# Attention and two mixtures on one core: K's two split parts on the two halves of one tile's partitions, Q doubled by DMA

## Chip, core and metric

The kernel runs on one core of a Trainium2 chip. The metric is the device time of one execution in microseconds. Before the change the median of 3 runs is 985.72 us (985.22 to 987.43).

## What is computed

Sliding-window attention with sinks (4 batches, 8 heads, 768 positions, 64 columns a head), then a layer of three competing products, then a routed mixture of eight experts:

```python
scores = q @ k.T / sqrt(64)                      # kept: first 4 positions, and the last 128 up to the own one
x = softmax(scores) @ v                          # 4 x 8 x 768 x 64, rearranged to 3072 x 512
x = max(x @ w1, x @ w2, x @ w3) @ w_out          # first mixture, 512 -> 768 -> 512
logits = x @ w_gate                              # 8 experts, room for 384 tokens each, greedy by logit
out[mask_e] = relu(x[mask_e] @ u1[e]) @ u2[e]    # second mixture, 512 -> 1024 -> 512
```

All inputs are float32.

## The kernel before

The attention is cut into 32 units: a batch, a half of its 768 positions, and a pair of heads (4 x 2 x 4). Four units make a group, one group of 384 tokens for the first mixture, eight groups in all. A unit goes through four functions: `load` (transfers of K, Q, V and the sinks, all issued on SP's queue), `prep` (lines 83 to 109), `score` (110 to 137) and `soft`, and `pv` (138 to 184). On the partitions lie the two heads of the pair, 64 rows each: head 0 on partitions 0 to 63, head 1 on 64 to 127. In the code `a` is a head's own half of the partitions, `o` the other half.

The first eight units are native: they use float32 matmuls as they are (L123) and nothing in `prep` but the sinks. The other 24 are split units. There each operand is cut into a rounded part (float32r) and a remainder, and a product is made as rounded times rounded, plus remainder times rounded, plus rounded times remainder. For the scores of a head before the change:

- `KH[h]` (tile kh) holds rounded K on both halves of the partitions: two copies on ACT (L94), from `u['kn']`.
- `KZ[h]` (tile kz, kz0b, kz1b) holds K's remainder on half `a`, zeros on half `o`: a subtract on DVE (L95). The zeros are written once, by POOL (L53).
- `QS[h]` (tile qs) holds rounded Q on half `a` (ACT, L96) and Q's remainder on half `o` (DVE, L97), from `u['qn']`.
- The scores (L126, L127) are two matmuls into one accumulator with the same stationary operand, a 128 x 128 slice of `QS[h]`: times `KH[h]`, then times `KZ[h]`. A unit has six such pairs (three query blocks, two heads), 24 units have 144 pairs. The moving operand has 260 columns, or 132 in a first block.

After that the scores go to the tile T by a copy on ACT (L134) and a masked copy on DVE (L130, L135); softmax follows on ACT, DVE and POOL; `pv` turns the probabilities on TensorE (L25), masks them on DVE (L163), splits them (L176 on ACT, L177 on POOL) and multiplies by V (L181, L182).

K tiles kh and kz have one buffer at first, and a second one after the sixth `o` step, when an extra pool becomes free (L659 to L662); qs has two throughout; kn and qn have one each, so the transfers for the next unit wait until `prep` has read them (L75 and L77 on SP's queue, then V and sinks, L79 and L81).

The first mixture: `group` (L280 on TensorE, L282, L283, L288, L289 on ACT and DVE) makes the hidden layer of a group, `x2` (L305) its output. The hidden layer of the first group is spilled to memory and read back by `reload` on SP's queue (L321), split again on ACT (L323) and DVE (L324), and multiplied in L305 between groups 1 and 2.

What sets the order: all of this stands in one block whose instructions a planner puts in order by a simulated timeline with estimated durations. The code gives it a sequence of steps (`order`, `order1`, `spread`) and higher priority to the units of the next group and to evacuations. Each engine and each queue then runs its own list strictly in that order. The second mixture (from 601 us) stands outside of this block.

## Time and profile before

| | |
|---|---|
| median of 3 runs | 985.72 us (985.22 to 987.43) |
| profiled execution, its own time | 985.81 us |
| its span in the trace | 984.0 us |
| TensorE matmuls busy | 937.8 us (95%), 6552 instructions |
| VectorE (DVE) | 687.8 us (70%) |
| ScalarE (ACT) | 533.8 us (54%) |
| GpSimd (POOL) | 348.8 us (35%) |
| SP's hardware queue | 40560 packets, 71.57 MB |
| chain that ended last | TensorE 75%, DVE 8%, ACT 6%, issue 5%, DMA 4% |

Lines such as L126 are lines of the kernel before. In the profile PE is TensorE, PEld its weight loads, and a releaser (`<-`) is what ended an idle time. Matmuls are pipelined: their recorded durations overlap, so that the distance between two of them is shorter than one of them. A chain lists, in order of time, the pieces of work that the end hung on.

### The profile page before, as it was taken

The page shows a single profiled execution, that of the slowest core. Times are in us where ns is not written, and L with a number is a line of the kernel's source. Part 1 is how long each engine was busy: PE and PEld are TensorE (multiplying, and loading weights), DVE is VectorE, ACT ScalarE, POOL GpSimd, SP SyncE. Part 2 cuts the span into 40 slices and gives each one's busy share as a digit, 9 for nine tenths or more (in the row PEclk, how much of TensorE's full clock was granted, in tenths as well). Part 3 has the DMA queues.
Part 4 walks back from the last instruction along what each step waited for, and adds up shares of the span by engine and source line. Part 5 has one row for each costly group of instructions (what it writes and reads, how often), then busy time and mean ns, then how long its engine had stood idle before and what let it go on. Part 6 is the DMA issues. An engine that isn't in the chain of part 4 may idle for free.

```text
span 984.0 us, 18469 instructions
## 1 busy us (share of the span) xinstructions
PE 937.8 (95%) x6552; PEld 857.8 (87%) x6552; DVE 687.8 (70%) x1807; ACT 533.8 (54%) x1425; POOL 348.8 (35%) x317
## 2 busy tenths in 40 slices
PE   5889999969999999999999999999999999999996
PEld 4568989959999999999999998888888888888895
DVE  3897676687879976776764344879989889873320
ACT  4666664788789777677663211233433434344431
POOL 3578357145555535425434000011113032043331
PEclk8899999989999999999999999999999999999999
DMA  7455121222112112112110002544345352454420
GB/s 226 151 170 172 50 77 64 68 83 88 53 40 78 52 49 73 28 48 81 64 50 12 1 1 76 164 154 130 119 149 174 98 172 99 160 189 154 135 81 32
DMA packets 50541, 95.03 MB, mean 97 GB/s; under 512 B 6704, under 2 KB 20784, under 8 KB 50448
## 3 DMA queue, kind: packets, MB, share of 16 engines
q1 hardware_dynamic: 40560, 71.57, 23.4%
q0 software_dynamic: 3840, 12.45, 3.6%
q10 hardware_dynamic: 6048, 9.83, 2.7%
q8 instruction: 51, 0.84, 0.4%
q14 instruction: 42, 0.34, 0.1%
HBM read 77.84 MB, written 16.12 MB: 95 GB/s over the span
## 4 chain that ended last, share of the span: by engine, by line
PE 75%; DVE 8%; ACT 6%; issue 5%; DMA 4%; POOL 1%; SPq 1%; POOLq 0%; ACTq 0%; DVEq 0%
PE mm L280 28%; PE mm L608 11%; PE acc L601 11%; PE mm L305 7%; PE po L181 3%; PE rc L406 2%; PE pt L25 2%; PE pp L25 2%; PE po L172 2%; PE ps L126 1%; PE ps L127 1%; DMA sa<-in_u_dram 1%; PE ps L123 1%; DVE A_w L163 1%; DVE qs L97 1%
## 5 line engine op out<-in xcount | busy, mean ns | idle before, releaser
L601 PE MATMUL acc<-wbh,HL 128*128 128x512 f32 x384 | 131.1, 398 | 0.0
L177 POOL TENSOR_TENSOR L<-A_w,H 128x768 fp32r<-128x768 f32 x46 | 87.0, 1891 | 101.5 <-ACT H L176 91.1
L283 DVE TENSOR_TENSOR hm<-mm,hm 128x384 f32<-128x384 f32 x96 | 53.3, 555 | 68.6 <-PE mm L280 65.1
L620 POOL DMA_INDIRECT out_dram<-og,idx x24 | 32.2, 1340 | 180.6 <-ACT og L619 177.3
L305 PE MATMUL mm<-woh,HL 128*128 128x260 f32 (+1 forms) x432 | 89.5, 296 | 2.0 <-DVE HL L324 1.1
L552 ACT ACTIVATE wah<-sa 128x512 fp32r<-128x512 f32 x64 | 40.5, 632 | 89.6 <-PE mm L608 72.2
L601 PEld LDWEIGHTS acc<-wbh,HL 128*128 128x128 f32 x384 | 71.5, 188 | 12.8
L552 ACT ACTIVATE wbh<-sb 128x512 fp32r<-128x512 f32 x64 | 40.4, 631 | 74.9 <-PE acc L601 72.0
L601 PE MATMUL acc<-wbl,HL 128*128 128x512 f32 x192 | 76.9, 401 | 0.0
L305 PEld LDWEIGHTS mm<-woh,HL 128*128 128x128 f32 x432 | 72.3, 198 | 3.3 <-DVE HL L324 1.4
L608 PE MATMUL mm<-HL,wah 128*128 128x384 f32 x256 | 68.5, 343 | 0.0
L280 PE MATMUL mm<-xh,w0h 128*128 128x384 f32 x192 | 66.8, 348 | 1.2 <-ACT xh L267 0.6
L280 PE MATMUL mm<-xh,w1h 128*128 128x384 f32 x192 | 66.7, 347 | 0.8 <-ACT hm L282 0.5
L280 PE MATMUL mm<-xl,w0h 128*128 128x384 f32 x192 | 65.5, 341 | 1.9 <-DVE xl L268 1.9
L280 PE MATMUL mm<-xh,w2h 128*128 128x384 f32 x192 | 67.0, 349 | 0.0
L280 PE MATMUL mm<-xh,w1l 128*128 128x384 f32 x192 | 65.5, 341 | 0.0
L280 PE MATMUL mm<-xl,w2h 128*128 128x384 f32 x192 | 65.5, 341 | 0.0
L553 DVE TENSOR_TENSOR wbl<-sb,wbh 128x512 fp32r<-128x512 f32 x64 | 43.9, 688 | 30.7 <-ACT wbh L552 30.7
L280 PE MATMUL mm<-xl,w1h 128*128 128x384 f32 x192 | 65.1, 339 | 0.0
L280 PE MATMUL mm<-xh,w0l 128*128 128x384 f32 x192 | 65.1, 339 | 0.0
L280 PE MATMUL mm<-xh,w2l 128*128 128x384 f32 x192 | 65.1, 339 | 0.0
L612 DVE SCALAR_TENSOR_TENSOR HL<-mm,HL 128x384 fp32r<-128x384 f32 x64 | 35.5, 554 | 40.8 <-ACT HL L611 40.6
(320 smaller groups left out, 2888.3 us busy)
## 6 DMA issues: line engine op xcount, KB each, us to landing
sa<-in_u_dram SPq DMA_DIRECT2D x64, 256.0 KB
sb<-in_u_dram SPq DMA_DIRECT2D x64, 256.0 KB
HL<-in_words_dram SPq DMA_DIRECT2D x18, 512.0 KB
qn<-in_q_dram SPq DMA_DIRECT2D x24, 192.0 KB
x2d<-xo ACTq DMA_DIRECT2D x15, 256.0 KB
kn<-in_k_dram SPq DMA_DIRECT2D x12, 264.0 KB
st<-in_words_dram SPq DMA_DIRECT2D x6, 512.0 KB
vn<-in_v_dram SPq DMA_DIRECT2D x12, 256.0 KB
```

The source lines that it names most:

```text
L25: nc.tensor.transpose(out,x,f32(ident))
L177: nc.gpsimd.tensor_tensor(L,Af,f32(H),op=OP.subtract)
L181: nc.tensor.matmul(po[:,q:q+n],u['VS'][:,blk,128*h:128*h+128],part[:,c:c+n],start=(part is H and j==0),stop=False,skip_group_check=True)
L280: nc.tensor.matmul(ps[:,:384],s.W[i][a][:,p,f*128:(f+1)*128],X[p][b],start=(n==0),stop=(n==11)); n+=1
L283: else: nc.vector.tensor_tensor(m,ps[:,:384],m,op=OP.max)
L305: nc.tensor.matmul(ps[:,:n],H[f][a][:,t*128:(t+1)*128],s.WO[b][:,f,u,c],start=(k==0),stop=(k==17)); k+=1
L552: nc.scalar.activation(h,src,AF.Copy)
L553: (nc.gpsimd if s.n>=6 and nm=="wa" else nc.vector).tensor_tensor(l,src,f32(h),op=OP.subtract)
L601: s.mms.append(nc.tensor.matmul(acc[t],H[f][a][:,t*128:(t+1)*128],W[f][1][b],start=(f==0 and n==0),stop=(f==F-1 and n==2))); n+=1
L608: s.mms.append(nc.tensor.matmul(ps[:,:384],W[f][0][a][:,k,:],X[k][b],start=(n==0),stop=(n==11))); n+=1
L612: nc.vector.scalar_tensor_tensor(l,ps[:,:384],0.0,f32(h),op0=OP.max,op1=OP.subtract)
L620: st=nc.gpsimd.indirect_dma_start(out=s.out,out_offset=bass.IndirectOffsetOnAxis(ap=idx[:,t:t+1],axis=0),in_=o,in_offset=None)
```

## The change

Rounded K and its remainder now stand in one tile `KK[h]` (the tiles kh): rounded on half `a`, by one ACT copy, and the remainder on half `o`, by the DVE subtract, which now writes across the halves. Q of a head is loaded twice, to both halves, so that one unit has four transfers of 64 x 384 in place of one of 128 x 384; one ACT copy over all 128 partitions rounds it into `QS[h]`. A new tile `QL[h]` holds Q's remainder on half `a` beside zeros on half `o`; it has one buffer at first and a second one after the sixth `o` step, as KZ had. The two matmuls of a pair now have the same moving operand, `KK[h]`, and two stationary ones, `QS[h]` and `QL[h]`. The zeros that POOL writes are 64 x 384 in place of 64 x 528. For native units only a name changes.

```diff
--- before.py
+++ after.py
@@ -44,7 +44,7 @@
         for i in range(2):
             t=consts.tile([128,2,128],FR,name=f"vk{i}"); nc.vector.memset(f32(t),0.0); s.vk.append(t)
             t=consts.tile([128,384],FR,name=f"psb{i}"); nc.vector.memset(f32(t),0.0); s.pb.append(t)
-        s.kf=[]; s.kz=[s.zeros([consts.tile([128,4,132],FR,name=f"kz{h}") for h in range(2)])]
+        s.kf=[]; s.ql=[s.zeros([consts.tile([128,384],FR,name=f"ql{h}") for h in range(2)])]
         t=consts.tile([1,1],FT,name="one"); nc.vector.memset(t,0.0)
         nc.scalar.activation(t,t,AF.Exp)
         s.n=0; s.no=('kh0','kh1')
@@ -65,16 +65,17 @@
         half=[(slice(64*h,64*h+64),slice(64-64*h,128-64*h)) for h in range(2)]
 
         if native:
-            u['KZ']=s.kf[u['n']%len(s.kf)]
-            for h,(a,o) in enumerate(half): nc.sync.dma_start(u['KZ'][h][a,:nb],s.k[i,a,:nb*132].rearrange("d (c j) -> d c j",j=132))
+            u['KK']=s.kf[u['n']%len(s.kf)]
+            for h,(a,o) in enumerate(half): nc.sync.dma_start(u['KK'][h][a,:nb],s.k[i,a,:nb*132].rearrange("d (c j) -> d c j",j=132))
             u['QF']=w.tile([128,384],FT,name="qf",tag="qs0",bufs=2)
             nc.sync.dma_start(u['QF'],s.q[i])
             u['vn']=w.tile([128,4,2,64],FT,name="vnn",tag="vsp")
         else:
             u['kn']=w.tile([128,4,132],FT,name="kn",bufs=1)
             nc.sync.dma_start(u['kn'][:,:nb],s.k[i,:,:nb*132].rearrange("p (c j) -> p c j",j=132))
-            u['qn']=w.tile([128,384],FT,name="qn",bufs=1)
-            nc.sync.dma_start(u['qn'],s.q[i])
+            u['qn']=[w.tile([128,384],FT,name=f"qn{h}",bufs=1) for h in range(2)]
+            for h,(a,o) in enumerate(half):
+                for r in (a,o): nc.sync.dma_start(u['qn'][h][r],s.q[i,a])
             u['vn']=w.tile([128,4,2,64],FT,name="vn",bufs=1)
         nc.sync.dma_start(u['vn'][:,:nb],s.v[i].rearrange("t (c h d) -> t c h d",h=2,d=64)[:,:nb])
         u['sv']=w.tile([40,2,64],FT,name="vns",bufs=1)
@@ -84,18 +85,18 @@
         nc=s.nc; w=s.w; nb=u['nb']; nat=u['nat']
         half=[(slice(64*h,64*h+64),slice(64-64*h,128-64*h)) for h in range(2)]
         if not nat:
-            KZ=s.kz[u['n']%len(s.kz)]
-            KH=[s.two(u,[128,4,132],FR,f"kh{h}") for h in range(2)]
+            KK=[s.two(u,[128,4,132],FR,f"kh{h}") for h in range(2)]
             QS=[w.tile([128,384],FR,name=f"qs{h}",bufs=2) for h in range(2)]
+            QL=s.ql[u['n']%len(s.ql)]
             fl=nb*132
             flat=lambda t: t.rearrange("p c j -> p (c j)")[:,:fl]
             for h,(a,o) in enumerate(half):
                 k=flat(u['kn'])[a]
-                for r in (a,o): nc.scalar.activation(flat(KH[h])[r],k,AF.Copy)
-                nc.vector.tensor_tensor(flat(KZ[h])[a],k,f32(flat(KH[h])[a]),op=OP.subtract)
-                nc.scalar.activation(QS[h][a,:],u['qn'][a],AF.Copy)
-                nc.vector.tensor_tensor(QS[h][o,:],u['qn'][a],f32(QS[h][a,:]),op=OP.subtract)
-            u.update(KH=KH,KZ=KZ,QS=QS)
+                nc.scalar.activation(flat(KK[h])[a],k,AF.Copy)
+                nc.vector.tensor_tensor(flat(KK[h])[o],k,f32(flat(KK[h])[a]),op=OP.subtract)
+                nc.scalar.activation(QS[h],u['qn'][h],AF.Copy)
+                nc.vector.tensor_tensor(QL[h][a],u['qn'][h][a],f32(QS[h][a]),op=OP.subtract)
+            u.update(KK=KK,QS=QS,QL=QL)
         VK=u['VK']=s.vk[u['n']%2]
         hi,lo=(bass.AP(tensor=VK.tensor,offset=VK.offset+o,ap=[[VK.ap[0][0],40],[st,2],[1,64]]) for o,st in (((0,64),(128,64)) if nat else ((0,192),(64,64))))
         nc.gpsimd.tensor_copy(hi,u['sv'])
@@ -119,12 +120,11 @@
             t=T[:,2*i:2*i+2,:].rearrange("p u j -> p (u j)")
             for h in range(2):
                 ps=s.pss.tile([128,512],FT,name="ps")
-                iq=slice(i*128,(i+1)*128); kz=u['KZ'][h].rearrange("p c j -> p (c j)")[:,lo:lo+n]
+                iq=slice(i*128,(i+1)*128); kz=u['KK'][h].rearrange("p c j -> p (c j)")[:,lo:lo+n]
                 if u['nat']: nc.tensor.matmul(ps[:,:n],u['QF'][:,iq],kz,start=True,stop=True)
                 else:
-                    kh=u['KH'][h].rearrange("p c j -> p (c j)")[:,lo:lo+n]
-                    nc.tensor.matmul(ps[:,:n],u['QS'][h][:,iq],kh,start=True,stop=False)
-                    nc.tensor.matmul(ps[:,:n],u['QS'][h][:,iq],kz,start=False,stop=True)
+                    nc.tensor.matmul(ps[:,:n],u['QS'][h][:,iq],kz,start=True,stop=False)
+                    nc.tensor.matmul(ps[:,:n],u['QL'][h][:,iq],kz,start=False,stop=True)
                 block=t[:,136*h:136*h+128]; sink=t[:,128+4*h:132+4*h]
                 if first:
                     nc.vector.copy_predicated(block,s.ca[:,0,:],ps[:,0:128])
@@ -659,7 +659,7 @@
                     if n==5:
                         conv.release()
                         A.extra=A_("extra",1,side="right"); A.no=('A',)
-                        A.kz.append(A.zeros([A.extra.tile([128,4,132],FR,name=f'kz{h}b') for h in range(2)]))
+                        A.ql.append(A.zeros([A.extra.tile([128,384],FR,name=f'ql{h}b') for h in range(2)]))
             for o in order.split(): emit(o,False)
             rest=None
             for g in range(NG):
```

## Rows read from the trace of the kernel before

**Rows 1.** busy time by stage: start:end, length, busy us and instructions of each engine, TensorE's clock, DMA

```profile
0.00:50.00 50.00, 35.21 (x137) 23.95 (x137) 31.16 (x81) 29.60 (x105) 22.96 (x37) 0.83 0.62 187
196.00:225.00 29.00, 20.77 (x120) 18.37 (x119) 25.93 (x44) 25.73 (x82) 13.51 (x9) 0.77 0.34 101
225.00:540.00 315.00, 311.29 (x2111) 305.80 (x2110) 229.43 (x431) 231.55 (x671) 146.87 (x124) 1.00 0.17 54
```

**Rows 2.** TensorE's waits from 196 to 225 us: total, times, longest

```profile
PE ps L126 <- DVE T_w L135: 4.3, 3, 2.0
PE pp L25 <- DVE A_w L163: 1.2, 1, 1.2
PE mm L305 <- DVE HL L324: 1.1, 1, 1.1
```

**Rows 3.** timeline of ACT from 196 to 225 us: start, duration, instruction, idle before

```profile
200.94 1.31 ACT L94 ACTIVATE kh_w<-kn 64x528 fp32r<-64x528 f32 x2
202.28 0.28 ACT L134 ACTIVATE T_w<-ps 128x132 f32<-128x132 f32 x1
```

**Rows 4.** timeline of DVE in the same stretch

```profile
201.62 1.50 DVE L95 TENSOR_TENSOR kz<-kn,kh_w 64x528 fp32r<-64x528 f32 x1 [0.22 <-ACT kh_w L94]
203.04 0.28 DVE L135 COPY_PREDICATED T_w<-ca,ps 128x128 f32<-128x128 uint8 x1
...
204.21 0.55 DVE L97 TENSOR_TENSOR qs<-qn,qs 64x384 fp32r<-64x384 f32 x1
...
212.63 0.55 DVE L324 TENSOR_TENSOR HL<-hm,HL 128x384 fp32r<-128x384 f32 x1
...
215.66 1.91 DVE L95 TENSOR_TENSOR kz0b<-kn,kh_x 64x528 fp32r<-64x528 f32 x1 [0.36 <-ACT kh_x L94]
```

**Rows 5.** chain that ended last, three pieces after the stall, one at 302 us

```profile
212.71 0.12 PE ps L127
212.83 0.12 PE ps L126
...
222.47 4.97 PE mm L305 x30
...
302.28 4.31 PE mm L305 x36
```

**Rows 6.** instructions by line and shape: busy us, mean ns, idle before

```profile
L96 ACT ACTIVATE qs<-qn 64x384 fp32r<-64x384 f32 x48 | 24.8, 517 | 0.6
...
L267 ACT ACTIVATE xh<-x 128x384 fp32r<-128x384 f32 x32 | 15.6, 517 | 4.0 <-PE mm L280 3.4 <-DVE x L184 0.4
L94 ACT ACTIVATE kh_x<-kn 64x528 fp32r<-64x528 f32 x24 | 15.4, 642 | 2.8 <-PE ps L126 2.4
L94 ACT ACTIVATE kh_w<-kn 64x528 fp32r<-64x528 f32 x24 | 15.4, 642 | 0.8 <-PE ps L126 0.4
...
L127 PEld LDWEIGHTS ps<-kz,qs 128*128 128x128 f32 x78 | 14.9, 191 | 0.0
L94 ACT ACTIVATE kh_w<-kn 64x396 fp32r<-64x396 f32 x28 | 14.9, 531 | 3.8 <-PE ps L126 3.4
...
L94 ACT ACTIVATE kh_x<-kn 64x396 fp32r<-64x396 f32 x20 | 10.7, 533 | 3.3 <-PE ps L25 1.7 <-PE ps L126 1.1
```

**Rows 7.** the page's DMA issues, Q of the split units

```profile
qn<-in_q_dram SPq DMA_DIRECT2D x24, 192.0 KB
```

**Rows 8.** timeline of SP's queue from 165 to 245 us

```profile
206.45 0.33 SPq L77 DMA_DIRECT2D qn<-in_q_dram  x1
208.67 2.44 SPq L321 DMA_DIRECT2D hm<-sp  x2
```

**Rows 9.** waits of SP's queue from 165 to 245 us: total, times, longest

```profile
SPq L321 <- DVE HL L324: 4.2, 2, 2.4
```

**Rows 10.** chain that ended last, its start

```profile
1.15 0.53 POOL kz L53
...
1.72 0.53 POOL kz L53
```

**Rows 11.** who waited for the transfers of line L321: us in total, times

```profile
  ACT HL L323: 2.1, 2
```

## The prediction

> **What bounds the kernel now.** I read four views in turn. First the busy time by stage [rows 1]: from 225 to 540 us, while the last split units run beside the first mixture, TensorE is busy 311.29 of 315 us at a granted clock of 1.00. There nothing that ACT, DVE or a queue does can be worth more than 3.7 us. One stretch of the attention work is different: from 196 to 225 us TensorE is busy 20.77 of 29 us and its granted clock is 0.77, while DVE is busy 25.93 and ACT 25.73 us. So I read who ended TensorE's waits there [rows 2]: 4.3 us go to the masked copies of the scores (L135), 1.2 us to L163, both DVE, and ACT or POOL end only small waits. Third, the two engines' timelines in that stretch [rows 3, 4]. ACT runs the two copies of rounded K back to back (1.31 us), and only then the score copy L134, which L135 must have. DVE in its turn starts each K subtract (L95) late, 0.22 and 0.36 us behind ACT's copy, and then needs 1.50 and 1.91 us. So in this stretch ACT and DVE hold each other up and TensorE stands behind both. Last, the chain of waits [rows 5]: 30 matmuls of L305 take 4.97 us (0.166 each) right after the stall, where 36 of them take 4.31 us (0.120 each) at 302 us. The stall thus costs twice, once in idle time and once in clock, which falls below the upper of its two levels, 2.4 GHz, after TensorE has stood.
>
> The first 50 us also leave TensorE idle (35.21 busy, clock 0.83 [rows 1]), but they belong almost wholly to the native units, which the change does not touch. From 601 us on the second mixture runs; its work and its instructions stay as they are.
>
> **The change, part by part.**
>
> *Removed on ACT.* Each split unit loses, per head, the second copy of rounded K. Of the 96 instructions of L94, 48 are 64x528 at 642 ns and 48 are 64x396 at 531 to 533 ns [rows 6]. Half go: 24 x 0.642 + 24 x 0.532 = 28.2 us of ACT. The copy of rounded Q grows from 64 to 128 partitions with the same 384 columns; L96 costs 517 ns on 64 partitions and L267 costs 517 ns on 128 [rows 6], so this is 0. Nearly all of the 28.2 us lies beside a busy TensorE [rows 1] and is worth nothing there. In the stretch from 196 to 225 us four of the copies that go are of the larger kind: 4 x 0.642 = 2.6 us. This is the upper bound of the gain. The lower bound is 0: the copies end at 202.25 us, but the L135 behind them starts at 203.04 us, when DVE is through with L95 [rows 3, 4]. I take half, 1.3 us, because ACT is nearly always busy in the stretch (25.73 of 29 us) and both L95 waited for it: whatever ACT sheds ahead of them reaches DVE, until DVE's own work ends last.
>
> *Clock.* If the stall shrinks, less work runs at the lower clock. The 30 matmuls above lost 30 x (0.166 - 0.120) = 1.4 us; bounds 0 and 1.4, taken 0.7.
>
> *Moved on DVE.* The K subtract writes to the other half of the partitions, the Q subtract now to its own; before it was the other way round. L97 crossed halves with 384 columns, L95 stayed with 396 or 528. The numbers of instructions and elements stay; an undisturbed L97, which crosses, takes 0.55 us, and so does L324, which does not, both with 384 columns [rows 4]. I take 0. Rounding leaves 0.01 us either way on each of 96 instructions, 1 us of DVE in all, of which the eight in the stretch (0.1 us) could show.
>
> *Waits.* The K remainder now waits for the earlier unit's score matmuls as the KZ write did, and the Q remainder, which earlier had two buffers, waits for them as well while there is only one QL pair, until the sixth o step is done. It stands in DVE's order behind the K subtract of the same head, which waits for the same matmuls of that head; so nothing new is queued behind it, 0. Later both tiles alternate between two buffers.
>
> *TensorE.* The score still takes two matmuls of the same size each, 288 in all. L127 has its own weight load of 191 ns although it uses the same stationary Q as L126 [rows 6], and in the chain a matmul of L126 that does change the stationary operand follows in 0.12 us, exactly as one of L127 that does not [rows 5]. So an operand that differs costs 0. A rule would speak against the change here: the Trainium skill, page "TensorE: Matmul & The Clock Gate", step "LDWEIGHTS" under "Step-by-step: what each phase is for", says that loads are separate so that one stationary operand can be loaded once and used by many matmuls. Where a compiler acted on that, the changed kernel would have new loads to pay; this trace disagrees, since each matmul already has its load. The price, had it been saved, is bounded by 144 x 0.19 = 27 us.
>
> *DMA and SP's queue.* One load of Q becomes four, of half the partitions each, and the bytes double from 192 to 384 KB [rows 7]. Each issue takes 0.33 us of SP's queue [rows 8], so 3 x 0.33 = 1.0 us more per unit, in front of V, the sinks, and everything SP issues later; in the stretch that is the reload of the spilled hidden layer (L321). What hides it there: the reload that was issued at 208.67 us, 2.2 us after the Q load at 206.45, waited for DVE's L324 to free its buffer, 4.2 us in two waits [rows 8, 9]. Bounds: 0, and 2 units x 1.0 us = 2.0 us if that cover is gone; taken 0. In the first 50 us the DMA moves 187 GB/s, so 192 KB more ahead of the words cost at most 192/187 = 1.0 us, once (the first split unit is loaded there); the load that the chain waits for there is issued ahead of it. Taken 0.
>
> *POOL.* Two zero fills shrink from 528 to 384 columns at the very start, where the chain of waits runs through POOL: 0.53 us [rows 10] x 144/528 = 0.15 each, 0.3 us. Bounds 0 and 0.3; taken 0.3.
>
> **The sum:** 1.3 + 0.7 + 0.3 = 2.3 us. The profiled execution took 985.81 us (span 984.0), 0.09 over the median of the runs, 985.72. 985.81 - 2.3 = 983.5; against the median 983.4. About 0.2% (2 us) is what a measurement of this kernel can tell from no change, so this is just beyond it.
>
> A second thing makes the bounds wide: the order of all this work is made by a planner from estimated durations. Shorter ACT work makes it deal out another order, and the 8.2 us of idle time in the stretch (29 - 20.77) plus 1.4 us of clock could be gone, or could come again at another place. So the order alone may move the time by up to 9.6 us either way.
>
> **The rivals.**
>
> *Relief where nobody waits* (no change). DVE, not ACT, ends the waits of L135 [rows 2, 4], and DVE sheds nothing. Then only POOL's 0.3 us and a little are left: 985.4 us. For it: DVE is the busier of the two in the stretch, if barely, and everywhere else TensorE is full. Against it: the two L95 that waited for ACT. Chance 0.32.
>
> *SP's queue takes its place* (slower). The four Q loads, issued together behind one release, push back the reload of the hidden layer. ACT's L323 already waits 2.1 us in two waits for those transfers [rows 11], and L305 1.1 us for the DVE step behind it [rows 2]. It decides from the point at which SP issues a reload later than DVE frees its buffer; it costs up to 2.0 us for the issues, as much again for the transfers behind 192 KB more, and the clock of a longer stall, 1.4 us: 985.7 + 2 to 5.4, about 989 us. Against it: the buffer, not SP, was late in the rows. Chance 0.12.
>
> *Another order* (slower): the planner's new order starves TensorE a second time, as between 196 and 225 us; half of 9.6 us gives 990 us. For it: a split unit's chain through four engines is long, and group starts need all four units. Against it: the 315 us after 225 us have almost no stall in spite of the same units. Chance 0.12.
>
> *Weights cost after all* (slower): the pair of matmuls shared a load in a way that the records hide. Up to 27 us, 1013 us. Against it stand the equal pitches [rows 5]. Chance 0.02.
>
> *The change isn't what it says*: if the planner kept the old order and all of it were covered, that is the first rival's time; it has no other share.
>
> **How the numbers follow.** My forecast, relief in the stall, has 0.42; its own range reaches from 976 (the whole stall of 9.6 us gone) to 983.7. No change has 0.32, slower 0.12 + 0.12 + 0.02 = 0.26. The range from 977 to 990 leaves out the tail beyond 990, the weights and the last of the gain, 2 in 10 at most. The predicted time is that of the likeliest case, 983.4.
>
> **What would show it.** Right: L94 with 48 instead of 96 instructions, Q's copy on 128 partitions still near 517 ns, TensorE's idle time between about 190 and 230 us below 8 us and its clock above 0.77, L323 waiting no longer than before. Wrong: a pitch of the second score matmul above 0.12 us; the crossing subtract longer than one of the same width that does not cross; L323 or the unit's own copies waiting for DMA; the same idle time in the stretch with ACT less busy (then DVE ended it); a new stretch in which TensorE stands and the clock falls.

## The result, and the profile after

The changed kernel takes 993.93 us (median of 7 runs, 989.2 to 997.52), the kernel before, in the same set, 987.43 us (7 runs, 985.22 to 991.46). The ratio is 1.0065, 95% interval 1.0037 to 1.0093: the change is **slower by 0.65%**, where 0.2% faster was forecast, and the time lies outside the range of 977 to 990. The profiled execution took 994.16 us, its span is 992.4 us.

The page of the changed kernel: busy time and share by engine, SP's hardware queue (packets, MB), the loads of Q.

```profile
PE 935.1 (94%) x6552; PEld 858.1 (86%) x6552; DVE 697.5 (70%) x1807; ACT 504.2 (51%) x1377; POOL 348.1 (35%) x317
...
q1 hardware_dynamic: 44784, 76.29, 25.0%
...
qn<-in_q_dram SPq DMA_DIRECT2D x96, 96.0 KB
```

ACT is 29.6 us less busy than before (533.8), where 28.2 us had been worked out. TensorE and POOL are busy as long as before within 3 us, DVE 9.7 us longer, and TensorE has the same 6552 matmuls to do in a longer span. Line numbers are one higher than before in the preparation (L95 and L96 are K's copy and subtract, L97 and L98 Q's) and up to the native score matmul (L124); from the score matmuls L126 and L127 on they are the same in both kernels.

Busy time by stage of the changed kernel (start:end, length, busy us of TensorE, its weight loads, DVE, ACT, POOL, then TensorE's clock, DMA share and GB/s); the first three answer to [rows 1].

```profile
0.00:50.00 50.00, 31.83 (x127) 21.98 (x129) 32.89 (x79) 28.23 (x102) 21.07 (x35) 0.86 0.65 196
196.00:225.00 29.00, 23.03 (x156) 20.65 (x155) 26.19 (x43) 22.96 (x75) 10.03 (x8) 0.94 0.38 112
225.00:540.00 315.00, 303.43 (x2040) 297.98 (x2039) 235.29 (x430) 209.79 (x642) 148.08 (x126) 0.98 0.21 64
...
260.00:310.00 50.00, 45.52 (x302) 44.59 (x301) 40.46 (x76) 31.27 (x96) 20.02 (x19) 0.93 0.20 58
380.00:455.00 75.00, 69.75 (x471) 68.62 (x471) 58.20 (x114) 49.13 (x149) 31.37 (x29) 0.98 0.19 60
```

The same view of the kernel before, from a second profile of it that was taken with the experiments (e8 below):

```profile
260.00:310.00 50.00, 48.72 (x347) 47.81 (x346) 44.18 (x84) 43.49 (x128) 23.59 (x21) 1.00 0.20 61
380.00:455.00 75.00, 74.19 (x512) 72.86 (x511) 50.61 (x102) 55.81 (x165) 32.00 (x28) 1.00 0.18 54
```

The stall of the prediction, 196 to 225 us, did shrink: idle time fell from 8.2 to 6.0 us and the clock rose from 0.77 to 0.94. But from 225 to 540 us, where TensorE had been full [rows 1], it now stands 11.6 us instead of 3.7, mainly in two places, and the granted clock falls below the upper level (2.4 GHz) in both, to 0.93 and 0.98 where e8 has 1.00.

Where the first mixture ends tells how much of the loss is whose. Its last matmul (L346) starts at 600.92 us before and at 610.67 us after. From there the spans go on for 383.1 and 381.7 us. So all of it, 9.8 us in these two profiles, is lost in the first 600 us. In a second pair (e8 and e5 below) it starts at 599.14 and 607.72 us, 8.6 us apart, and the spans go on for 391.1 and 392.6 us.

### The profile page after: what moved, and what is told of

Same layout as the page of the kernel before. It is cut to its first block, busy times and chain, and to the rows that moved or that the text cites. A ratio compares the mean times of both kernels' runs of the same rounds, so it can differ in the third digit from the quotient of the medians.

```text
span 992.4 us, 18541 instructions
## 1 busy us (share of the span) xinstructions
PE 935.1 (94%) x6552; PEld 858.1 (86%) x6552; DVE 697.5 (70%) x1807; ACT 504.2 (51%) x1377; POOL 348.1 (35%) x317
## 4 chain that ended last, share of the span: by engine, by line
PE 76%; DVE 8%; issue 5%; DMA 4%; ACT 4%; POOL 1%; SPq 1%; POOLq 0%; ACTq 0%; DVEq 0%
PE mm L280 29%; PE mm L608 11%; PE acc L601 11%; PE mm L305 7%; PE po L181 3%; PE rc L406 2%; PE pt L25 2%; PE pp L25 2%; PE ps L126 1%; PE ps L124 1%; PE po L172 1%; PE ps L127 1%; DMA sa<-in_u_dram 1%; DVE kh_w L96 1%; PE po L182 1%
## 5 line engine op out<-in xcount | busy, mean ns | idle before, releaser
L305 PE MATMUL mm<-woh,HL 128*128 128x260 f32 (+1 forms) x432 | 89.3, 296 | 2.8 <-DVE HL L324 1.2
L305 PEld LDWEIGHTS mm<-woh,HL 128*128 128x128 f32 x432 | 72.6, 199 | 3.9 <-DVE HL L324 1.4
L280 PE MATMUL mm<-xh,w0h 128*128 128x384 f32 x192 | 67.2, 350 | 0.5 <-DVE hm L283 0.5
L280 PE MATMUL mm<-xh,w2h 128*128 128x384 f32 x192 | 66.6, 347 | 1.1 <-ACT hm L282 1.1
L280 PE MATMUL mm<-xh,w1h 128*128 128x384 f32 x192 | 66.6, 347 | 0.8 <-ACT hm L282 0.5
L280 PE MATMUL mm<-xl,w0h 128*128 128x384 f32 x192 | 65.8, 343 | 0.8 <-DVE xl L268 0.8
L280 PE MATMUL mm<-xh,w1l 128*128 128x384 f32 x192 | 65.3, 340 | 0.0
L280 PE MATMUL mm<-xl,w2h 128*128 128x384 f32 x192 | 65.2, 340 | 0.0
L280 PE MATMUL mm<-xl,w1h 128*128 128x384 f32 x192 | 65.2, 339 | 0.0
L280 PE MATMUL mm<-xh,w0l 128*128 128x384 f32 x192 | 65.0, 338 | 0.0
L280 PE MATMUL mm<-xh,w2l 128*128 128x384 f32 x192 | 64.9, 338 | 0.0
```

What stands on the lines that cost most here:

```text
L280: nc.tensor.matmul(ps[:,:384],s.W[i][a][:,p,f*128:(f+1)*128],X[p][b],start=(n==0),stop=(n==11)); n+=1
L305: nc.tensor.matmul(ps[:,:n],H[f][a][:,t*128:(t+1)*128],s.WO[b][:,f,u,c],start=(k==0),stop=(k==17)); k+=1
```

## The experiments

Two theories were set against each other. **Loads theory**: the four half loads of Q cost time in any order, on SP's queue or by landing late. **Order theory**: the work is neutral, but the planner deals it out anew, and the new order starves TensorE at other places. A third question is whether ACT's relief is worth anything.

An order can be held. This function (shortened here), called at the end of the planned block, chains each engine's instructions (ORDER: one list per engine) by dependencies that carry no wait and fix only the order:

```diff
+def pin(tc):
+    ins=list(tc.nc.cur_bb.bb.instructions)
+    for d in ORDER:
+        last=None
+        for p in d:
+            if last is not None: tc.add_manual_dep(ins[p],last.name,NoSync,reason="order")
+            last=ins[p]
```

All results. Runs sent together shared a chip and the runs of the kernel before, to which each ratio refers. Its median was 992.67 us for e1 to e4b, 993.82 for e5 to e8, 985.97 for e9 to e12, 985.28 for e13 to e16, 986.14 for e17, 992.35 for e18.

| run | scores | Q loads | ACT copies of Q | order | ratio (95%) |
|---|---|---|---|---|---|
| the change | new | 4 | 2 | its own | 1.0065 (1.0037 to 1.0093) |
| e5, the change again | new | 4 | 2 | its own | 1.0089 (1.0061 to 1.0118) |
| e1 | new | 4 | 2 | old, units 9 to 12 re-placed | 1.0037 (1.0019 to 1.0055) |
| e17 | new | 4 | 2 | that of e13 | 1.0057 (1.0038 to 1.0075) |
| e18 | new | 4 | 4 | that of e13 | 1.0072 (1.0042 to 1.0101) |
| e13 | new | 1 | 4 | old, units 9 to 12 re-placed | 1.0005 (0.9985 to 1.0024) |
| e14 | new | 1 | 4 | free | 1.0040 (1.0019 to 1.0061) |
| e4 | old | 4 | 2 | old | 1.0027 (1.0010 to 1.0045) |
| e4b | old | 4 | 2 | free | 1.0296 (1.0268 to 1.0324) |
| e2 | old | 1 | 2 | that of the change, loads and preparation free | 1.0181 (1.0156 to 1.0207) |
| e15, e16 | new | 4 | 2 | lead 50, lead 70 | 1.0092 (1.0066 to 1.0119), 1.0078 (1.0049 to 1.0107) |
| e9 | new | 4 | 2 | its own, evictions first | 1.0068 (1.0044 to 1.0093) |
| e11 | new | 4 | 2 | old, evictions first | 1.0074 (1.0049 to 1.0099) |
| e10 | old | 1 | 2 | old, evictions first | 1.0120 (1.0091 to 1.0148) |
| e6, e7 | new, 64 rows | 4 | 2 | old, free | 1.0487 (1.0458 to 1.0515), 1.0358 (1.0323 to 1.0392) |
| e12 | new | 2, read twice | 2 | old, units 9 to 12 re-placed | 1.0489 (1.0457 to 1.0521) |

### Work and order exchanged: e1, e2, e5, e8

e1 is the changed kernel pinned to the order of before. The order can't be held for four units: in the plan of before DVE makes Q's remainder of units 9 to 11 ahead of the K subtract and of the scores of earlier units, which needs two buffers, and the one pair of QL tiles rules it out. Their loads and preparation were left to the planner.

> The changed kernel, its instructions held in the order of the kernel before on every engine and queue; only the loads and the prep of units 9 to 12 are left to the planner, since the single QL buffer cannot follow the old order there. Order theory (the loss is the planner's new order, the work itself is no dearer): 984 to 988 us, near before's 987.4, TensorE idle between 225 and 540 us about 4 us as before. Transfer theory (four Q loads cost the time, whatever the order): 992 to 996 us. Prep theory (the K subtract that crosses halves and the QL waits cost it): 991 to 995 us.

e2 is the reverse: before's work in the order of the change, with the loads and preparation of its split units left to the planner.

> The kernel before, with score, softmax, PV and the whole first mixture held in the order of the changed kernel (TensorE's order is the changed kernel's throughout); loads and prep of the split units are left to the planner. Order theory: as slow as the change, 991 to 997 us, or more, since ACT has 28 us more to do. Transfer theory and prep theory: 986 to 989 us, as before.

e5 and e8 are the two kernels as they are. They came to another chip than e1 and e2, against what their expectations say; before takes nearly the same on both (993.82 and 992.67 us).

> The changed kernel itself, on the chip of the first four experiments, so that it can be set beside them. Order theory (what the change costs is the new order of the work in the first 600 us): its ratio to before lies clearly above that of the new work in the old order (1.0037), at 1.005 to 1.009, 998 to 1002 us where before is at 993. Loads theory (the four Q loads cost the same in any order): the same ratio as the new work in the old order and as the loads alone, 1.002 to 1.005, 995 to 998 us.

> The kernel before, unchanged, for one profile on the same chip: 0.997 to 1.003 of itself. It is a scale for reading the other profiles: in the part from 604 us on, where all kernels have the same instructions in the same order, the first four experiments lost 5 to 12 us to low clock and stalls against the profile of before that was taken on another chip; both theories expect this profile to show a loss of that kind too, 2 to 12 us, which then belongs to the chip and the execution and not to an edit.

Measured: e1 1.0037, e2 1.0181, the change (e5) 1.0089; e8 took 992.02 us. The interval of e1 lies below that of e5, but overlaps that of the change's first runs (1.0037 to 1.0093); so it is likely, and not settled, that the change's own order costs something. e1 isn't at 1.000 either, so the order is not all. e2 shows that before's work fits the change's order worse than the new work does, but it is no clean reversal: with its loads re-placed, one K load alone makes TensorE wait 5.5 us. e8 lines up with the first profile of before within 2 us up to the last L346 (599.14 against 600.92 us), and then takes 8.0 us longer for the same instructions: differences of that size behind 600 us arise without any edit. This is why the profiles below are compared up to that matmul.

The stretch of the prediction in e1 (busy time by stage):

```profile
196.00:225.00 29.00, 19.30 (x119) 17.20 (x119) 26.40 (x41) 22.11 (x73) 11.48 (x8) 0.85 0.31 93
```

ACT is relieved there too, 22.11 us busy instead of 25.73, and TensorE stands as long as before the change (9.7 us; 8.2 in [rows 1], 8.9 in e8). So ACT's relief alone does not shrink the stall. The order of the change without the relief (e2, ACT busy 25.30 us) leaves 7.3 us, the order with it 6.0 us in the first profile of the change and 4.3 in e5. The order is thus needed; whether the relief adds to it is not separated, since e2's loads are placed anew.

### The loads: e4, e4b, e13, e14, e17, e18

e4 is the kernel before in its own order, but with Q by four half loads, two of them into a tile of 320 columns instead of 384 that nobody reads; e4b is the same with the planner free.

```diff
-            nc.sync.dma_start(u['qn'],s.q[i])
+            qd=w.tile([128,320],FT,name="qd",bufs=1)
+            for h,(a,o) in enumerate(half):
+                nc.sync.dma_start(u['qn'][a],s.q[i,a]); nc.sync.dma_start(qd[o],s.q[i,a,0:320])
```

> The kernel before, in its own order, with four Q loads in place of one: two halves as before, and two more halves, 320 columns wide, that nothing reads. Order theory: 986 to 989 us, the loads are hidden (SP has 1 to 1.4 us more per unit). Transfer theory: 991 to 995 us. Prep theory: 986 to 989 us.

> The same four loads in the kernel before, but the planner free to make its own order. Order theory: another order and with it another time than e4's, by some us; no sign can be given, 985 to 997 us, and more than 2 us from e4. Transfer theory: as e4, 991 to 995 us. Prep theory: as before, 986 to 989 us.

e13 takes the extra loads out of the change: Q comes in one load, and ACT writes its rounded copy to both halves. e14 is e13 with the planner free.

```diff
-                nc.scalar.activation(QS[h],u['qn'][h],AF.Copy)
-                nc.vector.tensor_tensor(QL[h][a],u['qn'][h][a],f32(QS[h][a]),op=OP.subtract)
+                for r in (a,o): nc.scalar.activation(QS[h][r],u['qn'][a],AF.Copy)
+                nc.vector.tensor_tensor(QL[h][a],u['qn'][a],f32(QS[h][a]),op=OP.subtract)
```

> The change's scores (rounded Q against both parts of K on one tile, the remainder of Q beside zeros), but Q is loaded once, as before, and ACT writes its rounded copy to both halves (four copies of 64 partitions per unit in place of two of 128); held in the order of before, with the loads and preparation of units 9 to 12 re-placed as in the first experiment. ACT has its old work again, SP and the DMA queues too. Loads theory: without the four loads the 0.37% of the first experiment goes, 0.998 to 1.002. Order theory (what is left in the first experiment is the re-placing of units 9 to 12 that one pair of remainder tiles forces): 1.002 to 1.005 as there.

> The same kernel with the planner free. Its TensorE order has 2663 of 3459 instructions in the order of before, as far off as the change's. Order theory: 1.003 to 1.03, over the same kernel in the old order by 0.003 or more, with new waits in the first 600 us. Loads theory: within 0.002 of the same kernel in the old order.

e17 holds the changed kernel in the order of e13, all units; e18 is e17 with four ACT copies of 64 partitions, as e13 has.

> The changed kernel, every instruction of the first part on every engine held in the order that the kernel with one Q load and ACT's doubling has in its run in the old order (units 9 to 12 too). Against that kernel (1.0005, 0.9985 to 1.0024) it differs only in that four half loads stand where one load stood, and two ACT copies where four stood. Loads theory: 1.003 to 1.005, and TensorE's losses against that kernel arise where a Q tile or another load lands later. Rival (the loads are harmless, and the 0.37% of the first experiment came from how units 9 to 12 were placed): 0.997 to 1.001, the relief of ACT being worth at most 0.3%.

> The missing corner: four half loads as in the change, but ACT makes the rounded Q in four copies of 64 partitions as in the kernel with one load (each half from its own loaded half), all in that kernel's order. Against e13 (one load, four copies, 1.0005) it adds only the loads; against e17 (four loads, two copies, 1.0057) it adds only ACT work, 48 copies of 0.52 us. Loads theory: 1.004 to 1.007, as e17, and ACT's 25 us make no difference. Rival (not the loads, but the earlier ends of ACT's copies shift DVE against POOL): 0.999 to 1.002, as e13. If the relief of ACT is worth something after all, the time lies above e17, 1.007 or more.

Measured: e13 1.0005, e17 1.0057, e18 1.0072. These three have the same order, and only the two with four loads are slow: **the loads cost 0.52%** from e13 to e17, 5.1 us, with an uncertainty of about 0.27% (the two intervals' half widths, added in squares), and 0.67% from e13 to e18, which differ in the loads and their tiles alone. ACT's Q copies make no difference that can be measured: ACT is busy 504.8 us in e17 and 527.4 in e18, and e17 is 0.15% faster with an uncertainty of 0.35%. e18 stands just above the 1.007 from which its expectation would have called ACT's relief worth something, so that a gain of 1 or 2 us is neither shown nor excluded. The kernel before with such loads (e4) loses 0.27% in its own order. So the loads theory holds, and by these medians for the greater part of the loss.

A free order can cost something too: with one load, it costs 0.35% over the held one, with an uncertainty of 0.29% (e14, e13), and the same loads that cost 0.27% in the old order cost 2.96% in the order that the planner made for them (e4, e4b). For the change itself no such cost is measured: with four loads the held orders give 1.0037, 1.0057 and 1.0072 (e1, e17, e18), its own 1.0065 and 1.0089.

Where the loads are seen: the timeline of SP's queue in the changed kernel (Q is L78, the reload L321), to set beside [rows 8].

```profile
187.62 2.61 SPq L78 DMA_DIRECT2D qn<-in_q_dram  x4
...
207.31 2.64 SPq L321 DMA_DIRECT2D hm<-sp  x2
```

The line of these loads, by tile, in the changed kernel (duration in ns min/median/max, first and last start):

```profile
L78 SPq DMA_DIRECT2D qn<-in_q_dram x96: 465/476/1725, 17.0 to 468.8; - x96
```

One issue took 0.33 us before (median 328 ns); one of a half load takes 0.476 us at the median and four of them together 2.61 us at 187.62. SP is held 1.6 to 2.3 us longer per unit, not 1.0. In the first 50 us, where the prediction set the loads at nothing, the chain of waits of the changed kernel now runs through a Q load:

```profile
22.52 3.72 DMA qn<-in_q_dram
```

and that of e17 through another, between 190 and 200 us, where that of e13 has none:

```profile
193.39 4.79 DMA qn<-in_q_dram
```

Neither is a fixed price. The chain of e5, the changed kernel again, runs through no Q load before 600 us, and neither does that of e18.

TensorE's matmuls stand in the same order in e13, e17, e18 and e1, so their starts can be compared one by one. Behind the load at 193.39 us e17 falls 1.0 us further behind e13, e18 only 0.1 us. What e17, e18 and e1 share are two other places, and at both TensorE waits for DVE: the L25 that starts at 223.00 us in e13 comes 1.2 to 1.4 us further behind, the L280 that starts at 482.66 us 1.6 us. Together they are most of what e18 has lost by the last L346 (3.1 us: 603.63 against 600.53 us), half of e1's loss (5.7 us) and a third of e17's (8.2 us, of which 2.1 us arise in the first 40 us, where two profiles of the kernel before differ by 1.9 us). e4, with the old scores, loses nothing against the kernel before at either. That four loads cost about 5 us in the changed kernel is shown by the medians. Whether the issue, the landing or the second Q tile brings these waits about, no run takes apart.

### DVE's subtracts beside POOL: e9, e10, e11

The two new stalls have the same picture. The timeline of DVE, POOL and TensorE in the changed kernel (start, us, instruction, idle before it and what ended it):

```profile
300.16 2.15 DVE L96 TENSOR_TENSOR kh_w<-kn,kh_w 64x528 fp32r<-64x528 f32 x1
302.34 0.56 DVE L98 TENSOR_TENSOR ql<-qn,qs 64x384 fp32r<-64x384 f32 x1
302.93 0.30 DVE L135 COPY_PREDICATED T_w<-ca,ps 128x128 f32<-128x128 uint8 x1
303.26 0.70 DVE L96 TENSOR_TENSOR kh_w<-kn,kh_w 64x528 fp32r<-64x528 f32 x1
...
449.08 3.42 DVE L98 TENSOR_TENSOR ql1b<-qn,qs 64x384 fp32r<-64x384 f32 x1
452.53 0.30 DVE L135 COPY_PREDICATED T_w<-ca,ps 128x128 f32<-128x128 uint8 x1
...
299.95 1.80 POOL L177 TENSOR_TENSOR L<-A_w,H 128x768 fp32r<-128x768 f32 x1 [2.92 <-PE mm L305]
...
447.86 1.80 POOL L177 TENSOR_TENSOR L<-A_w,H 128x768 fp32r<-128x768 f32 x1
449.63 1.50 POOL L147 TENSOR_TENSOR T_x<-T_x,l 128x792 f32<-128x792 f32 x1
...
303.28 0.58 PE L126 MATMUL ps<-kh_x,qs 128*128 128x260 f32 x1 [2.66 <-DVE T_w L135]
...
452.88 0.58 PE L126 MATMUL ps<-kh_w,qs 128*128 128x260 f32 x1 [2.53 <-DVE T_w L135]
```

A K subtract of the next unit takes 0.70 us when POOL stands and 2.15 us when it begins during an operation of POOL; a Q subtract takes 0.56 or 3.42 us. Both stand in DVE's list ahead of the masked copy (L135) that frees the accumulator TensorE waits for. The Trainium skill, page "SBUF — State Buffer", section "Who interferes with whom", states that a DVE instruction with two SBUF inputs contends with a GpSimd instruction that reads SBUF; the trace agrees, and its price in the lines shown here and below is 1.2 to 2.9 us a time.

From this came a sharper theory: put the evictions (the masked copies L135 that empty the accumulator) first. In DVE's list each subtract that stands directly ahead of an eviction of an earlier unit's scores was moved behind it, in the change (e9), in before (e10) and in e1 (e11). Schematically, for unit n and the next one:

```diff
-  QL0(n+1), evict(n), KK1(n+1), QL1(n+1), evict(n)
+  evict(n), evict(n), QL0(n+1), KK1(n+1), QL1(n+1)
```

> The changed kernel in its own order on every engine, but on DVE a subtract of K's or Q's remainder that stands directly ahead of an eviction of an earlier unit's scores is moved behind that eviction (95 exchanges of neighbours, 22 units); nothing else differs. DVE theory: in the change's order these subtracts, stretched to 1.8 to 3.4 us where POOL works beside them (297.3, 391.3, 397.9 and 445.9 us in the second profile of the change), hold up the evictions that TensorE waits for, and the clock falls after it. Then the wait of the score matmul for the eviction L135 drops from 8 or 9 us to about 4, the two low stretches of 6.8 us near 298 and 448 us go, and the ratio is 0.997 to 1.003, against 1.0089 for the change. Rival: the subtracts that come later make the next unit's scores late by as much, or the work is short of something else; 1.006 to 1.011.

> The same exchange in the kernel before, in its own order otherwise (63 exchanges, 22 units). DVE theory: the kernel before has the same fault in a lesser degree (its wait of the score matmul for the eviction is 5.3 us in 5 places), so 0.995 to 1.000. Rival (its stalls come from elsewhere, the stretch 196 to 225 us above all): 1.000, or slower where a subtract comes late, up to 1.004.

> The changed kernel in the order of before as in the first experiment (four units' loads and preparation re-placed), with the same exchange on DVE (55 exchanges, 21 units). DVE theory: 0.997 to 1.002, against 1.0037 without it. Loads theory: the 0.27% of the loads alone stays, 1.002 to 1.005.

Measured: 1.0068, 1.0120 and 1.0074. The theory fell. TensorE's waits from 40 to 600 us, first in the changed kernel, then in e9 (total, times, longest):

```profile
PE ps L126 <- DVE T_w L135: 9.2, 9, 2.7
```

```profile
PE mm L305 <- ACT xo L307: 2.6, 4, 1.0
...
PE mm L280 <- DVE hm L283: 2.3, 3, 1.0
PE ps L126 <- DVE T_w L135: 2.2, 4, 0.7
```

The wait for L135 went as expected, from 9.2 to 2.2 us, and came back elsewhere: L305 and L280 wait 2.6 and 2.3 us where they had waited 1.0 and 0.5, and the last L346 starts at 609.19 us, 1.5 us earlier than in the first profile of the change and 1.5 us later than in the second. In before the same exchange takes its wait from 5.3 us (e8) to 2.8 us and the whole is 1.2% slower. From 225 to 540 us DVE is at work 235 of 315 us in e9; the likely reading, which no run tests further, is that a subtract that is put off is late for something else. So these places are where the loss shows, and this exchange does not mend them.

Why such small edits move so much can be read from two kernels in the same order, at the first of the two places that the four loads make late. DVE, POOL and TensorE in e13:

```profile
221.25 0.70 DVE L95 TENSOR_TENSOR kh_x<-kn,kh_x 64x528 fp32r<-64x528 f32 x1
221.98 0.96 DVE L162 TENSOR_TENSOR A_w<-pp,ul 128x768 f32<-128x768 f32 x1
...
220.75 0.61 POOL L101 CAST vk<-vns 40x128 fp32r<-40x128 f32 x1
221.38 1.70 POOL L109 TENSOR_TENSOR vsp<-vn,vsp 128x512 fp32r<-128x512 f32 x1
...
223.00 0.55 PE L25 MATMUL pp<-ident,T_w 128*128 128x128 f32 x3 [1.59 <-DVE A_w L162]
```

The same instructions in e17:

```profile
224.60 1.91 DVE L96 TENSOR_TENSOR kh_x<-kn,kh_x 64x528 fp32r<-64x528 f32 x1
226.53 0.96 DVE L163 TENSOR_TENSOR A_w<-pp,ul 128x768 f32<-128x768 f32 x1
...
224.10 0.61 POOL L102 CAST vk<-vns 40x128 fp32r<-40x128 f32 x1
224.68 1.25 POOL L110 TENSOR_TENSOR vsp<-vn,vsp 128x512 fp32r<-128x512 f32 x1
...
227.55 0.90 PE L25 MATMUL pp<-ident,T_w 128*128 128x128 f32 x3 [2.79 <-DVE A_w L163]
```

The K subtract begins 0.50 us behind the cast in both. POOL's next operation begins 0.63 us behind the cast in the one and 0.58 us in the other, and which of the two had to wait was reversed: POOL (1.70 us) in e13, DVE (1.91 us) in e17. A shift of 0.05 us lies between two outcomes that are 1.2 us apart, ahead of an instruction that TensorE waits for. It is no throw of one execution: in e18 POOL's operation begins 0.58 us behind the cast as in e17, and the K subtract takes 1.91 us.

At the second place it is a Q subtract, first in e13, then with the matmul behind it in e17:

```profile
480.57 0.56 DVE L97 TENSOR_TENSOR ql1b<-qn,qs 64x384 fp32r<-64x384 f32 x1
```

```profile
486.70 2.13 DVE L98 TENSOR_TENSOR ql1b<-qn,qs 64x384 fp32r<-64x384 f32 x1
...
490.36 0.44 PE L280 MATMUL mm<-xh,w0h 128*128 128x384 f32 x1 [1.68 <-DVE hm L283]
```

In e18 it takes 2.15 us. The kernel before has the first place as e13 has it (0.70 us) and the second as e17 (2.12 us), though TensorE waits only 0.35 us for it there.

### How far the order alone goes: e15, e16

```diff
-def attention_mixtures(...,off=60,...)
+def attention_mixtures(...,off=50,...)
```

(70 in e16.)

> The changed kernel with one number of the planner's input altered: attention is put 50 instructions ahead in priority, not 60. No instruction is added or removed. Order theory: the planner finds another order and the time moves by up to 3% either way, 0.995 to 1.035; it shows how far the order alone moves this work. Loads theory: 1.004 to 1.009 as in the change, since the loads are the same.

> The changed kernel with attention 70 instructions ahead. As with 50: order theory 0.995 to 1.035 and different from both 50 and 60, loads theory 1.004 to 1.009.

Measured: 1.0092 and 1.0078. With other orders, the change stays at 1.0065 to 1.0092. That speaks for a cost that the change has in any order and against an unlucky throw of the planner; the 3% that the order theory allowed did not come.

### Two ways around that cost more: e6, e7, e12

e6 and e7 put both heads' Q remainders into one tile without zeros, so that the second matmul contracts only the 64 partitions of the head. One tile is half the memory, two buffers fit, and the order of before is possible for every unit (e6); e7 is free.

```diff
-            QL=s.ql[u['n']%len(s.ql)]
+            QL=w.tile([128,384],FR,name="ql",bufs=2)
...
-                    nc.tensor.matmul(ps[:,:n],u['QL'][h][:,iq],kz,start=False,stop=True)
+                    a=slice(64*h,64*h+64); nc.tensor.matmul(ps[:,:n],u['QL'][a,iq],kz[a],start=False,stop=True)
```

> The changed kernel, but the Q remainders of both heads share one tile of two buffers, each on its own 64 partitions, without zeros: the second matmul of a score contracts the 64 partitions that hold the remainder. With two buffers the order of before is possible for every unit, and every instruction in the first part is held in it; no unit is exempt as in the first experiment. Same four loads, same ACT and DVE work as the change. Order theory: all that was wrong with the change is gone, ACT has 28 us less, so 0.996 to 1.001 of before, 988 to 993 us. Loads theory: still 1.002 to 1.005, 995 to 998 us, as with the loads alone. A third outcome, the halved contraction is dearer on TensorE: the pitch of the second score matmul above 0.12 us and 1.005 or more.

> The same kernel, with the planner free to order it. Order theory: the planner finds yet another order (2588 of 3459 TensorE instructions in the order of before), and the time can land anywhere from 0.995 to 1.03, with the difference to the kernel in the old order arising in single stalls of the first 600 us. Loads theory: within 0.003 of the kernel in the old order.

Measured: 1.0487 and 1.0358, the third outcome. TensorE's timeline of six score matmuls in e6, then of before (e8):

```profile
339.45 0.38 PE L127 MATMUL ps<-kh_x,ql 64*128 64x260 f32 x1
339.77 0.39 PE L126 MATMUL ps<-kh_x,qs 128*128 128x260 f32 x1
340.08 0.38 PE L127 MATMUL ps<-kh_x,ql 64*128 64x260 f32 x1
```

```profile
312.56 0.28 PE L127 MATMUL ps<-kz,qs 128*128 128x260 f32 x1
312.68 0.28 PE L126 MATMUL ps<-kh_w,qs 128*128 128x260 f32 x1
312.80 0.28 PE L127 MATMUL ps<-kz,qs 128*128 128x260 f32 x1
```

From start to start 0.31 to 0.32 us instead of 0.12. So these two runs tell nothing about the order; they show what the zeros are worth.

e12 keeps four half tiles filled but issues two loads per unit, each reading its 64 rows twice:

```diff
-                for r in (a,o): nc.sync.dma_start(u['qn'][h][r],s.q[i,a])
+                src=s.q[i,a]; nc.sync.dma_start(u['qn'][h],bass.AP(tensor=src.tensor,offset=src.offset,ap=[[0,2]]+[list(x) for x in src.ap]))
```

> The changed kernel in the order of before as in the first experiment, but each doubled Q tile is filled by one DMA that reads its 64 rows twice: two Q loads per unit instead of four, the same bytes, the same tiles and the same work. If the issuing on SP (0.47 us for one half load) is what the loads cost: 1.000 to 1.003. If the bytes or the landing are: as with four loads, 1.002 to 1.006. If the cost is not the loads at all but DVE: also 1.002 to 1.006, with the same waits of TensorE as in the first experiment.

Measured: 1.0489, outside all three. The line of the loads, and how long the engines that use their tile waited for them (us, times):

```profile
L78 SPq DMA_DIRECT2D qn<-in_q_dram x48: 503/520/603, 16.6 to 490.9; - x48
...
  DMA qn<-in_q_dram: 35.7, 17
```

The two issues are shorter than four (1.04 instead of 1.9 us), but the engines stood 35.7 us in 17 waits for the landing, against 2.6 us in 2 in the changed kernel. What makes these loads late is not shown. The question whether SP's issuing or the landing makes up the 5 us is not answered by this run, and stays open.

No version beat the kernel before. e13, with Q loaded once and ACT doing the doubling, equals it (1.0005).

## Why the prediction was wrong

The step that failed is **DMA and SP's queue**: "Bounds: 0, and 2 units x 1.0 us = 2.0 us if that cover is gone; taken 0", and the same 0 for the first 50 us. It looked for the price in one stretch and at one waiting instruction. That instruction behaved as predicted; who waited for the reload (L321) in the changed kernel, beside [rows 11]:

```profile
  ACT HL L323: 1.2, 2
```

But 24 units carry the loads, and in a held order they cost 5.1 us (e13 to e17). The two losses that e17, e18 and e1 share are waits of TensorE for DVE, at a K and a Q subtract beside POOL, 1.2 to 1.4 and 1.6 us; the prediction had no term for a load that shifts DVE against POOL. How the loads shift them stays open. The issue was mis-sized as well: 0.476 us for a half load, taken at 0.33 from the whole one.

The rival "SP's queue takes its place" (chance 0.12) named the loads, and its 2 to 5.4 us hold the measured 5.1; but its path, a late reload, is not the one that the runs show, so that its number is right by luck.

The other steps:

- **Removed on ACT**, 1.3 us: not borne out. Over the whole run nothing can be measured (e17 against e18, 0.15% with an uncertainty of 0.35%, where 1.3 us are 0.13%), and in the old order the stretch from 196 to 225 us is as idle as before (e1). That speaks for the rival "relief where nobody waits": DVE ended those waits. The size of the work removed was sound (29.6 us measured), and so was Q's copy over 128 partitions: 516 ns against 519 over 64 (medians). **Clock**, 0.7 us, hangs on this term and is not shown either.
- The sign by which the step was to be confirmed, less idle time in the stretch, came true in the changed kernel (6.0 us, clock 0.94), but not by ACT's relief alone: in the old order it did not come (e1, 9.7 us). Without the held order it would have passed as proof. One of the prediction's signs of being wrong came true beside it: new stretches in which TensorE stands and the clock falls, near 300 and 450 us.
- **Waits**, 0: wrong in its ground. It took the text's order for DVE's. In the plan of before, DVE makes Q's remainder of three units well ahead, out of two buffers; with one QL pair it can't, and these units' loads and preparation must be placed anew. The price of that alone is small: e13 has it and is at 1.0005 (0.9985 to 1.0024).
- **Another order** (a rival, chance 0.12, 990 us): the order did change, and may account for what the loads leave. 0.35% with one load (e14 against e13); for the change itself the difference between its own and a held order is 0.3 to 0.5% against e1 and not measurable against e17 and e18. The two new stalls are this rival's: in e17 the longest such wait is 1.9 us, as in e13. e17, which has no such stall, is within the uncertainty as slow as the change.
- **Moved on DVE**, 0: right. The K subtract that crosses halves takes 564 ns at least and 703 or 704 at the median; before, 554 at least and, tile by tile, 696, 904 and 706 at the median. The 9.7 us more on DVE are not the price of crossing: e13 has the same subtracts, and DVE is busy 686.8 us in it, 687.8 before.
- **TensorE**, 0: right. In both profiles of the change the pitch of the two score matmuls is 0.12 us, as before, and in the first L127 has its own weight load of 192 to 194 ns on average, 189 to 194 before.
- **POOL**, 0.3 us: about right; the two zero fills take 0.41 instead of 0.53 us each, 0.24 us together. A difference of this size can't be seen in the time of the whole.

## What to carry to other kernels

Price a load by all the units that carry it, not at the one place where a wait is visible; doubling data by DMA to save work on an engine that TensorE did not wait for was a loss here. Where a planner orders the work, a change of any instruction changes the order, and a confirmation in one stretch proves little: hold the old order, exchange work and order, and compare up to the last instruction that the change can reach. In this kernel operations of DVE and POOL that meet in SBUF turned a shift of 0.05 us into more than 1 us of waiting on TensorE, which is as much as the gain that was worked out on paper.

## What the runs showed that was not expected

- Alternating contractions of 128 and 64 partitions on TensorE costs 0.19 us at every change (pitch 0.31 instead of 0.12 us, in e6); with 144 such matmuls, two changes each, that is up to 144 x 2 x 0.19 = 55 us, and 48 us were measured in e6, 36 in e7. The Trainium skill, page "TensorEngine Tiling (Array Packing)", section "Key Properties", states that a change of the tiling mode drains TensorE; the trace agrees and gives the price.
- A DMA that reads the same 64 rows twice is issued faster than two half loads (0.520 us against twice 0.476), but its readers wait far longer for it: 35.7 us in e12 against 2.6 us in the changed kernel.
- The two profiles of the kernel before agree within 2 us up to the last L346 and then take 383.1 and 391.1 us for the same instructions. This goes with the chip: the part behind the last L346 took 380 to 388 us in the profiles taken where the kernel before runs in 985 to 987 us, and 387 to 395 us where it runs in 992 to 994 us. What makes the chips differ is open.
